# Second part of the query product units at later positions, one unit product ahead of the score tiles, two last-group steps joined

## The chip, the cores and the metric

The kernel runs on one core of one Trainium2 chip. The metric is the device time of one execution in microseconds (us). All times in this document are in us unless marked ns.

## What is computed

The inputs are x (2048 rows of 512), a key and a value cache for 32 heads of 128 columns, the projections wq (512 by 4096) and wo (4096 by 512), and the three weights of a gated block with 1792 inner columns. All are bf16.

```python
xn = layernorm(x)                                        # no scale, no offset
q  = (xn @ wq)   as 32 heads of 128
s  = softmax(q k_cache^T / sqrt(128)) @ v_cache          # all 2048 keys, no mask
s  = s as 2048 x 4096 @ wo
g  = silu((relu(xn @ W_gate) * (xn @ W_up)) @ W_down)
out = x + s * g
```

## The kernel before

**The main loop.** Attention is cut into 128 blocks: 32 heads (h) by 4 quarters of 512 query rows (Q), in that order. A block has 8 positions (p = 0 to 7). A position stands for one pair of key tiles, 256 keys. At each position TensorE (PE) runs two score tiles `S` (L1466, 128x512 each) of a pair three positions ahead, and eight products `PV` with the values (L1575, 128x129 each) of the present pair. ScalarE (ACT) turns each score pair into `PT` by one exp (L1478). The loop in L1761 to L1815 writes this out by hand: the order in which it emits instructions is the order in which each engine runs them, and nothing is reordered later. I write "block 26, position 4" as 26.4; as the loop is in L1762 to L1765, 26.4 emits the scores for the block position three further on (26.7) and the values of 26.4.

**The score ring.** `ps_r` has three slots of two PSUM banks. `ring_acquire` takes the slot at the front of the list, puts it at the back, and makes PE wait for the last reader of that slot. A score pair is read by its exp; another product by VectorE (DVE). A unit (below) holds a slot: the slot leaves the list until `ring_release` puts it back in second place, and meanwhile the score pairs rotate through the two others. The value products accumulate in `ps_acc`. At the end of a block DVE takes the reciprocal (L1495) and writes the normalized block (`Onorm`, L1498); the first value product of the next block waits for that.

**Other products at fixed positions.** `plan` maps (block, position) to groups of products that are emitted there between the score tiles and the value products. `side` does the same for work on other engines. What is in them in the part that the change touches:

- *Query product units* (`emit_unit`, L1019). From group 2 of four heads on, q is computed by a seven-product scheme of two nested levels. A unit is one outer product of one group; there are 7 units in each of 6 groups, 42 in all. Unit k of group g starts in block b = 16(g-1) + 5 + 2k and takes the outer products j = 1, 2, 6, 5, 3, 7, 4 in turn. It has six steps. Steps 0 to 3 stand in block b at positions 2, 3, 5, 6, or at 3, 4, 6, 7 where b is an "early" block; they hold one ring slot. Steps 4 and 5 are the second part: one 128x512 product each (L1032), at positions 2 and 4 of block b + 1, holding a slot again. Each product is added to sums by DVE (L1036, L1037).
- *Adds of a unit* (`add_unit`, L1095). After the second part of the units with j = 5 and j = 7, GpSimd (POOL) does four adds (L1103), which wait for the last DVE sum of that unit. The first DVE sum of the next unit's step 0 waits for these adds (`k.get("add")`, L1060, L1063), and PE's step 1 waits for that sum (L1066).
- *Preparation of a unit* (`prep_unit`, L992). POOL makes the eight sums that a unit multiplies; it waits for step 5 of the unit two before (`u_done`).
- *Output projection steps* (`emit_os`, L1326). 16 steps in the 16 blocks after each group, at position 0: three steps of two products, then a step of one product, four times over (each product is four 128x256 matmuls, L1347). DVE adds them to `s_acc` (L1363, L1365). The block of a one-product step is early (`early`, 24 such blocks in groups 2 to 7 that follow the second part of a unit, and 119): at position 0 PE emits the next two score pairs and then the step, which needs a third slot. Four DVE sums `OX` over SBUF (`emit_ox`, L1316 to L1324) serve four steps at a time; they stand at positions 2 to 5 of every eighth block, 24 and 32 for example.
- *The last group's steps* have been pulled together: steps 0 to 9 at blocks 112 to 121, steps 10 and 11 at 122.0 and 122.4, then 123.0, 124.0, 125.0 and 125.4. After each one-product step DVE finishes two sums (L1413, L1415), and `emit_base_next` (two DVE operations, L1443 and L1448) puts in the residual and g for each of 16 row tiles.

Of the kernel before, what the change touches and what calls it, by code (L numbers as in the profile page):

```python
# [30 lines left out]
def _wait(eng, tok):  # L31
    if tok is None:
        return
    sem, val = tok
    if val <= 0:
        return
    eng.wait_ge(sem.h, val)
# [15 lines left out]
def bass_recurrent_scan__mha_block_cached__glu_gated_reglu__prompt_kernel(  # L53
# [24 lines left out]
    NP = KT // 2  # L78
# [3 lines left out]
    NG = H // G  # L82
# [34 lines left out]
    with ExitStack() as es:  # L117
# [232 lines left out]
        def issue_wq(pr):  # L350
            b = pr % 2
            src = A_wq[:, pr * 2 * Dh:(pr + 1) * 2 * Dh].rearrange("(c p) e -> p c e", p=128)
            sem_wq[b].sig(sp.dma_start(Wq_sb[b][:].rearrange("p c i e -> p c (i e)"), src))
# [35 lines left out]
        def ring_acquire(hold=False):  # L389
            s = ring_order.pop(0)  # L390
            if not hold:
                ring_order.append(s)
            _wait_all(pe, ring_tok[s])
            ring_tok[s] = []
            return s
# [450 lines left out]
        def blk_of(gp):  # L846
            b, p = divmod(gp, NP)
            h, Q = divmod(b, QB)
            return b, h, Q, p

        def emit_M(items):
            if items[0][0] is emit_unit:
                emit_unit(*items[0][2:])
                return
            s = ring_acquire()
            toks = []
            k = 2 * s
            for fn, nb, *args in items:
                t = fn(*args, *range(k, k + nb))
                toks += t if isinstance(t, list) else [t]  # L860
                k += nb
            ring_tok[s] = toks
# [13 lines left out]
        def emit_st(pr, c, step, *banks):  # L876
# [57 lines left out]
            if c == 1:  # L934
# [6 lines left out]
        unit_at = [(g, j, GBK * (g - 1) + 5 + 2 * k) for g in range(2, NG)  # L941
                   for k, j in enumerate((1, 2, 6, 5, 3, 7, 4))]
        u_prep = {}
        u_done = {}
        u_tok = {}
        u_held = {}
# [338 lines left out]
        def emit_wx_scale(g):  # L1285
            W = Wo_sb[g % 2]
            _wait(pool, wo_tok(g))
            wflat = W[:].rearrange("p h d -> p (h d)")
            k = sem_wx.sig(pool.tensor_scalar(wflat, wflat, WOSC, None, op0=ALU.mult))
            wx_tok[(g, 0)] = k  # L1290
# [141 lines left out]
        def issue_xr(k):  # L1432
            n = base_order[k]
            if k >= 4:
                _wait(sp, base_done[base_order[k - 4]])
            sem_xr[k % 4].sig(sp.dma_start(xr_sb[:, k % 4:k % 4 + 1, :], x_t[:, n:n + 1, :]))
# [17 lines left out]
        def open_S_pair(gp):  # L1454
            b, h, Q, p = blk_of(gp)
            if p == 0:
                _wait(pe, qt_ready[(h, Q)])
                if Q == 0:
                    _wait(pe, kt_tok(h))
            s_slot[gp] = ring_acquire()  # L1460

        def emit_S_tile(gp, tt):
            b, h, Q, p = blk_of(gp)
            s = s_slot[gp]
            t = 2 * p + tt
            ins = pe.matmul(ps_r[:, 2 * s + tt, :], KT_sb[h % 2][:, t * 128:(t + 1) * 128],  # L1466
                            QT_sb[qt_slot[(h, Q)]][:], start=True, stop=True)
            if tt == 0:
                return
            stok = sem_s.sig(ins)  # L1470
            if p == NP - 1:
                qt_free.append((qt_slot[(h, Q)], stok))
                if Q == QB - 1:
                    shead_tok[h] = stok
            _wait(act, stok)
            pb = gp % NPB
            etok = sem_exp.sig(
                act.activation(PT[pb][:], ps_r[:, 2 * s:2 * s + 2, :], ACTF.Exp,  # L1478
                               scale=scale / WSC)
            )  # L1480
            assert etok[1] == gp + 1
            ring_tok[s] = [etok]
# [106 lines left out]
        def sp_head_start(h):  # L1589
            if h + 1 < H:  # L1590
                _wait(sp, shead_tok.get(h - 1))
                issue_kt(h + 1)
# [48 lines left out]
        def at(b, p, *items):  # L1641
            plan.setdefault((b, p), []).append(list(items))
# [4 lines left out]
        LB = NBLK - QB  # L1647
        side = {}
        osteps = {}
        early = set()  # L1650
        for g in range(NG - 1):
            b0 = (g + 1) * GB
            for i in range(16):
                it = (emit_os, 1 if i % 4 == 3 else 2, g, i // 4, i % 4)
                if g < NG - 2 or i < 10:
                    osteps[b0 + i] = it
                else:
                    at(b0 + (10, 10, 11, 12, 13, 13)[i - 10], 4 * (i in (11, 15)), it)
            for c in range(2):
                for i in range(4):  # L1660
                    side.setdefault((b0 + 7 * c, 1 + i) if c and g == NG - 2 else (b0 + 8 * c, 2 + i), []).append((emit_ox, g, c, i))
# [20 lines left out]
        for b in range(NBLK):  # L1682
            pr, r = (b - 2) // 8 + 1, (b - 2) % 8
# [22 lines left out]
            elif 0 < pr < NPR:  # L1706
                c, step = r // 4, r % 4
                q = (emit_st, 1 if step == 3 else 2, pr, c, step)
                first, second = (o, q) if step == 3 and o else (q, o)
# [4 lines left out]
                assert not o  # L1714
        for n, (g, j, b) in enumerate(unit_at):
            first = (3, 4, 6, 7) if b in early else (2, 3, 5, 6)
            for step, (r, p) in enumerate([(0, p) for p in first] + [(1, 2), (1, 4)]):
                at(b + r, p, (emit_unit, 0, n, step))
            side.setdefault((b - 2, 0), []).append((prep_unit, n))
            if j in (5, 7):  # L1720
                side.setdefault((b + 1, 5), []).append((add_unit, g, j))
        side.setdefault((GB + 1, 0), []).append((spill_g,))
        side.setdefault((LB - 9, 5), []).append((reload_g,))
        for g in range(2, NG):
            b = GB * (g - 1)
            side.setdefault((b + 2, 0), []).append((load_unit_w, g, 0))
            side.setdefault((b + 2, 6), []).append((scale_unit_w, g, 0))
            b, p = (21, 6) if g == 2 else (b + 4, 0)
            side.setdefault((b, p), []).append((load_unit_w, g, 1))
            b, p = (22, 4) if g == 2 else (b, 3)  # L1730
            side.setdefault((b, p), []).extend([(scale_unit_w, g, 1), (sum_unit_w, g)])
        base_at = [(LB - 7 + k // 2, 2 + k % 2) for k in range(4)]
        base_at += [(LB - 4 + k // 2, 2 + k % 2) for k in range(4)]
        base_at += [(LB - 1 + k // 2, 2 + k % 2) for k in range(4)]
        base_at += [(LB + 2, 2), (LB + 2, 5), (LB + 3, 1), (LB + 3, 3)]
        for bb, pp in base_at:
            side.setdefault((bb, pp), []).append((emit_base_next,))
# [6 lines left out]
        def emit_S_pair(gp):  # L1744
            open_S_pair(gp)
            emit_S_tile(gp, 0)
            emit_S_tile(gp, 1)
# [13 lines left out]
        for gp in range(LAG, TOTP):  # L1761
            gq = gp - LAG  # L1762
            bq, hq, Qq, pq = blk_of(gq)
            items = plan.pop((bq, pq), None)
            b, h, Q, p = blk_of(gp)  # L1765
            if p == 0 and Q == 0:
                sp_head_start(h)
            ahead = gp in s_ahead
            if not ahead:
                open_S_pair(gp)  # L1770
                emit_S_tile(gp, 0)
            if pq == 0 and bq % 8 == 4:
                pr = bq // 8 + 2
                if pr < 4:
                    _wait(sp, qp_done_tok[pr - 2])
                    issue_wq(pr)
            if pq == 4 and bq % 8 == 4:
                pr = bq // 8 + 2
                if pr < 4:
                    emit_sw(pr)  # L1780
            if pq == 0 and bq == (NG - 1) * GB + 4:
                _wait(sp, u_tok["last"])
                for k in range(4):
                    issue_xr(k)
            if pq == 4 and bq == 0:
                gu_sums(2)
            if pq == 0 and bq == 13:
                emit_wx_scale(0)
            if pq == 0 and bq == GB:
                emit_wx(0)  # L1790
            if pq == 0 and bq == GB + 4:
                emit_wx(1)
            if pq == 6 and bq % GB == 7 and 1 < bq // GB < NG - 1:
                emit_wx(bq // GB)
            if items:
                if not ahead:
                    emit_S_tile(gp, 1)
                if pq == 0 and bq in early:
                    s_ahead.add(gp + 1)
                    emit_S_pair(gp + 1)  # L1800
                for it in items:
                    emit_M(it)
            for fn, *args in side.pop((bq, pq), []):
                fn(*args)
            for fn in later.pop(gq, []):
                fn()
            now[0] = gq + 1
            split = not items and not ahead
            if split and (u_held or (pq == NP - 1 and bq + 1 in early)):
                emit_S_tile(gp, 1)  # L1810
                split = False
            emit_PV_tile(gq, 0)
            if split:
                emit_S_tile(gp, 1)
            emit_PV_tile(gq, 1)  # L1815
# [41 lines left out]
```

## Time and profile before

| what | value |
|---|---|
| median of 3 runs | 1254.27 (1254.26 to 1254.38) |
| the profiled execution's own time | 1254.29 |
| its span | 1252.9 |
| mean granted TensorE clock | 0.999 |
| PE matmul busy | 1233.0 (98%) |
| ACT busy | 1033.4 (82%) |
| DVE busy | 811.0 (65%) |
| POOL busy | 596.2 (48%) |

The span runs from the first to the last instruction of the program; the 1.4 us between span and time lie around it. A row of the timeline gives the start, the time from the first start to the last end, the engine, the line, what is written from what, and the count; in square brackets stands the idle time of that engine before it, with what ended it in the profiler's view. PEld is the loading of weights, which runs one matmul ahead of PE. A row of the waits gives who waited for whom, the sum, the count and the longest.

### The profile page before, as it was taken

The page shows a single profiled execution, that of the slowest core. Times are in us where ns is not written, and L with a number is a line of the kernel's source. Part 1 is how long each engine was busy: PE and PEld are TensorE (multiplying, and loading weights), DVE is VectorE, ACT ScalarE, POOL GpSimd, SP SyncE. Part 2 cuts the span into 40 slices and gives each one's busy share as a digit, 9 for nine tenths or more (in the row PEclk, how much of TensorE's full clock was granted, in tenths as well). Part 3 has the DMA queues.
Part 4 walks back from the last instruction along what each step waited for, and adds up shares of the span by engine and source line. Part 5 has one row for each costly group of instructions (what it writes and reads, how often), then busy time and mean ns, then how long its engine had stood idle before and what let it go on. Part 6 is the DMA issues. An engine that isn't in the chain of part 4 may idle for free.

```text
span 1252.9 us, 29140 instructions
## 1 busy us (share of the span) xinstructions
PE 1233.0 (98%) x12125; PEld 857.2 (68%) x12353; DVE 811.0 (65%) x1328; ACT 1033.4 (82%) x1109; POOL 596.2 (48%) x606
## 2 busy tenths in 40 slices
PE   9999999999999999999999999999999999999998
PEld 5466666776677676767667676667666776777775
DVE  7677877665576746575665747574666647674667
ACT  4457877668888898889898898889889898889994
POOL 3373876415734367344845366534835466430002
PEclk9999999999999999999999999999999999999999
DMA  9712331323122232323122333233222232235312
GB/s 273 155 31 39 77 77 23 54 45 107 43 48 52 69 65 52 52 64 69 41 38 39 72 61 51 48 69 68 48 51 49 45 58 48 52 64 144 76 35 77
DMA packets 254914, 82.25 MB, mean 66 GB/s; under 512 B 226368, under 2 KB 254784, under 8 KB 254784
## 3 DMA queue, kind: packets, MB, share of 16 engines
q1 hardware_dynamic: 254112, 79.98, 30.6%
q8 instruction: 98, 1.61, 0.5%
q10 hardware_dynamic: 672, 0.39, 0.1%
q14 instruction: 32, 0.26, 0.1%
HBM read 40.63 MB, written 4.19 MB: 36 GB/s over the span
## 4 chain that ended last, share of the span: by engine, by line
PE 80%; ACT 10%; issue 8%; DVE 1%; POOL 0%; DMA 0%; POOLq 0%; DVEq 0%
PE ps_acc L1575 31%; PE ps_r L1466 25%; ACT PT L1478 10%; PE ps_r L1347 6%; PE ps_r L1032 6%; PE ps_r L1144 3%; PE ps_r L1205 3%; PE ps_r L711 2%; PE ps_r L715 2%; PE ps_r L896 2%; PE ps_acc L814 1%; POOL g_sb L1630 0%; DMA x_sb<-in_A_x_dram 0%; PE ps_r L528 0%; DVE stats L406 0%
## 5 line engine op out<-in xcount | busy, mean ns | idle before, releaser
L1478 ACT ACTIVATE PT<-ps_r 128x1024 bf16<-128x1024 f32 x1024 | 982.0, 1030 | 150.4 <-PE ps_r L1466 142.4
L1575 PEld LDWEIGHTS ps_acc<-V_sb,PT 128*128 128x128 bf16 x8192 | 579.3, 98 | 202.4 <-ACT PT L1478 2.9
L1575 PE MATMUL ps_acc<-V_sb,PT 128*128 128x129 bf16 x8192 | 697.9, 220 | 5.6
L1466 PE MATMUL ps_r<-QT_sb,KT_sb 128*128 128x512 bf16 x1834 | 613.0, 379 | 5.0 <-DVE QT_sb L901 0.3
L1037 DVE TENSOR_TENSOR UVR<-UVR,ps_r 128x512 f32<-128x512 f32 (+1 forms) x228 | 166.3, 756 | 91.3 <-PE ps_r L1032 86.8
L1365 DVE TENSOR_TENSOR s_acc<-s_acc,ps_r 128x512 f32<-128x512 f32 x264 | 167.6, 682 | 21.5 <-PE ps_r L1347 21.5
L1466 PEld LDWEIGHTS ps_r<-QT_sb,KT_sb 128*128 128x128 bf16 x2048 | 175.6, 98 | 7.6 <-ACT PT L1478 0.5
L1495 DVE RECIPROCAL rz_sb<-ps_acc 128x4 f32<-128x4 f32 x127 | 23.0, 181 | 186.2 <-PE ps_acc L1575 185.3
L1498 DVE TENSOR_TENSOR Onorm<-ps_acc,rz_sb 128x512 bf16<-128x512 f32 x127 | 87.8, 692 | 4.4
L1004 POOL TENSOR_TENSOR TI<-xn_sb 128x512 f16<-128x512 f16 x48 | 58.0, 1209 | 68.0 <-PE ps_r L1032 68.0
L978 POOL TENSOR_SCALAR Wq_sb<-Wq_sb 128x1024 bf16<-128x1024 bf16 x12 | 33.2, 2769 | 118.3 <-DMA Wq_sb<-in_A_wq_dram 118.3
L1037 DVE TENSOR_TENSOR QT_sb<-UVR,ps_r 128x512 bf16<-128x512 f32 x72 | 49.5, 688 | 36.2 <-PE ps_r L1032 33.2
L1004 POOL TENSOR_TENSOR TI<-xnT 128x512 f16<-128x512 bf16 x36 | 41.6, 1156 | 64.2 <-PE ps_r L1032 63.4
L1103 POOL TENSOR_TENSOR QT_sb<-UVR,UVR 128x512 bf16<-128x512 f32 x24 | 34.8, 1481 | 72.7 <-DVE UVR L1037 72.7
L1630 POOL TENSOR_TENSOR g_sb<-s_acc,WX 128x512 bf16<-128x512 f32 x6 | 6.8, 1154 | 124.1 <-DVE WX L1623 124.1
L1103 POOL TENSOR_TENSOR UVR<-UVR,UVR 128x512 f32<-128x512 f32 x24 | 29.7, 1269 | 72.6 <-DVE UVR L1037 72.6
L1004 POOL TENSOR_TENSOR TI<-xn_sb,TI 128x512 f16<-128x512 f16 x48 | 55.3, 1152 | 0.0
L1032 PE MATMUL ps_r<-TI,SI 128*128 128x512 f16 x126 | 48.2, 382 | 0.6
L1347 PE MATMUL ps_r<-WX,OX 128*128 128x256 f16 x336 | 45.8, 273 | 0.0
L1004 POOL TENSOR_TENSOR TI<-xnT,TI 128x512 f16<-128x512 bf16 x36 | 41.6, 1156 | 0.0
L1120 POOL TENSOR_SCALAR gB<-gB 128x512 bf16<-128x512 bf16 x14 | 20.8, 1487 | 42.6 <-DVE gB L1150 42.6
L1347 PEld LDWEIGHTS ps_r<-WX,OX 128*128 128x128 f16 x336 | 32.8, 98 | 9.8 <-ACT PT L1478 1.8
(186 smaller groups left out, 1193.9 us busy)
## 6 DMA issues: line engine op xcount, KB each, us to landing
V_sb<-in_A_v_cache_dram SPq DMA_DIRECT2D x32, 512.0 KB, 4.3
Wq_sb<-in_A_wq_dram SPq DMA_DIRECT2D x16, 256.0 KB, 3.1
Wo_sb<-in_A_wo_dram SPq DMA_DIRECT2D x8, 512.0 KB, 4.1
out_dram<-g_sb SPq DMA_DIRECT2D x4, 512.0 KB, 4.8
g_sb<-out_dram SPq DMA_DIRECT2D x4, 512.0 KB, 6.4
xr_sb<-in_A_x_dram SPq DMA_DIRECT2D x16, 128.0 KB, 2.2
OT_store<-Onorm SPq DMA_TRANSPOSE x127, 2.5
Wd_sb<-in_B_W_down_dram SPq DMA_DIRECT2D x1, 1792.0 KB, 14.0
```

The source lines that it names most:

```text
L1004: return sem_ui.sig(pool.tensor_tensor(dst, x, y, o))
L1032: return sem_up.sig(pe.matmul(dst, lhs, rhs, start=start, stop=stop, skip_group_check=True))
L1037: dve.tensor_tensor(dst, x, ps, ALU.add))
L1103: u_tok["add"] = sem_uv.sig(pool.tensor_tensor(dst, UU[:, i, :], RR[:, i, :], ALU.add))
L1144: ins = pe.matmul(ps_r[:, bank, :], L(i), R(i), start=(i == 0), stop=(i == HC - 1))
L1205: ins = pe.matmul(ps_r[:, bank, j * DH:(j + 1) * DH], L(i), R(i), start=(i == 0 and j == 0), stop=(i == HF - 1 and j == 1))
L1347: ins = pe.matmul(ps_r[:, bank, j * DH:(j + 1) * DH], L(i), R(i), start=(i == 0 and j == 0), stop=(i == GH - 1 and j == 1))
L1365: t = dve.tensor_tensor(names[k], names[k], view(bank), op)
L1466: ins = pe.matmul(ps_r[:, 2 * s + tt, :], KT_sb[h % 2][:, t * 128:(t + 1) * 128], QT_sb[qt_slot[(h, Q)]][:], start=True, stop=True)
L1478: act.activation(PT[pb][:], ps_r[:, 2 * s:2 * s + 2, :], ACTF.Exp, scale=scale / WSC)
L1498: dve.tensor_tensor(Onorm[ob][:], o_ap, rz_sb[:].to_broadcast([128, 4, Dh]), ALU.mult))
L1575: ins = pe.matmul(o_ap, PT[pb][:, tt, j * 128:(j + 1) * 128], V_sb[vb][:, t, 0:VW], start=(t == 0 and j % 2 == 0), stop=(t == KT - 1 and j ...
```

## The change

1. The second part of each unit (steps 4 and 5) moves from positions 2 and 4 of block b + 1 to 5 and 7 where b + 2 is early, and to 3 and 5 elsewhere.
2. In early blocks that begin a unit, step 3 (position 7) is emitted before the score tiles of that position, not after them. The score pair there is then split around the value products like a plain one.
3. In the last group, the one-product step 7 no longer has block 119 to itself. Steps 8 to 10 move one block earlier, and step 7 is emitted with the one-product step 11 at 122.0 in one slot. Block 119 is thereby no longer early. Eight of the 16 `emit_base_next` calls move with them: from 120.2, 120.3, 121.2, 121.3, 123.2, 123.3, 124.2, 124.3 to 122.3, 122.5, 123.2, 123.3, 123.5, 124.2, 124.3, 124.5.

No instruction is added or taken away.

```diff
+        ahead_of_S = set()
...
             for i in range(16):
                 it = (emit_os, 1 if i % 4 == 3 else 2, g, i // 4, i % 4)
-                if g < NG - 2 or i < 10:
-                    osteps[b0 + i] = it
+                k = (0, 1, 2, 3, 4, 5, 6, None, 7, 8, 9, 10, 11, 12, 13, 13)[i] if g == NG - 2 else i
+                if k is None:
+                    late = it
+                elif g < NG - 2 or i < 10:
+                    osteps[b0 + k] = it
                 else:
-                    at(b0 + (10, 10, 11, 12, 13, 13)[i - 10], 4 * (i in (11, 15)), it)
+                    at(b0 + k, 4 * (i == 15), *([late] if i == 11 else []), it)
...
             first = (3, 4, 6, 7) if b in early else (2, 3, 5, 6)
-            for step, (r, p) in enumerate([(0, p) for p in first] + [(1, 2), (1, 4)]):
+            second = (5, 7) if b + 2 in early else (3, 5)
+            for step, (r, p) in enumerate([(0, p) for p in first] + [(1, p) for p in second]):
                 at(b + r, p, (emit_unit, 0, n, step))
+            if first[3] == NP - 1:
+                ahead_of_S.add(b)
...
-        base_at += [(LB - 4 + k // 2, 2 + k % 2) for k in range(4)]
-        base_at += [(LB - 1 + k // 2, 2 + k % 2) for k in range(4)]
+        base_at += [(LB - 2, 3), (LB - 2, 5), (LB - 1, 2), (LB - 1, 3), (LB - 1, 5), (LB, 2), (LB, 3), (LB, 5)]
...
             ahead = gp in s_ahead
+            if pq == NP - 1 and bq in ahead_of_S:
+                for it in items:
+                    emit_M(it)
+                items = None
             if not ahead:
                 open_S_pair(gp)
                 emit_S_tile(gp, 0)
```

## The prediction

> **What bounds the kernel now.** I read the page first (busy shares, chain), then the waits, then the timeline of single block boundaries.
>
> ```profile
> PE 1233.0 (98%) x12125; PEld 857.2 (68%) x12353; DVE 811.0 (65%) x1328; ACT 1033.4 (82%) x1109; POOL 596.2 (48%) x606
> PE 80%; ACT 10%; issue 8%; DVE 1%; POOL 0%; DMA 0%; POOLq 0%; DVEq 0%
> PEld ps_r L1347 <- ACT PT L1478: 18.4, 43, 0.7
> ```
>
> PE is busy for 98% of the span, and no matmul is removed. So only PE's short waits can move the time. The largest in the changed part is the third row: 43 times the weights of an output projection step wait for an exp, because the step's ring slot still holds a score pair. The sum of 18.4 overstates it, since weights load one matmul ahead. What PE itself loses is read at one boundary, 26 to 27:
>
> ```profile
> 372.76 0.59 PE L1466 MATMUL ps_r<-QT_sb,KT_sb 128*128 128x512 bf16 x2
> 373.20 0.62 PE L1575 MATMUL ps_acc<-V_sb,PT 128*128 128x129 bf16 x8
> 373.65 1.03 PE L1466 MATMUL ps_r<-QT_sb,KT_sb 128*128 128x512 bf16 x4
> 374.76 0.61 PE L1347 MATMUL ps_r<-WX,OT_store 128*128 128x256 f16 x4
> 375.21 0.28 PE L1575 MATMUL ps_acc<-V_sb,PT 128*128 128x129 bf16 x2
> ...
> 373.85 0.18 DVE L1495 RECIPROCAL rz_sb<-ps_acc 128x4 f32<-128x4 f32 x1 [2.42 <-PE ps_acc L1575]
> 374.07 0.69 DVE L1498 TENSOR_TENSOR Onorm<-ps_acc,rz_sb 128x512 bf16<-128x512 f32 x1
> ...
> 367.88 3.77 ACT L1478 ACTIVATE PT<-ps_r 128x1024 bf16<-128x1024 f32 x4 [0.70 <-PE ps_r L1466]
> 371.85 3.77 ACT L1478 ACTIVATE PT<-ps_r 128x1024 bf16<-128x1024 f32 x4 [0.20 <-PE ps_r L1466]
> ...
> 370.33 0.38 PE L1032 MATMUL ps_r<-TI,SO 128*128 128x512 f16 x1
> 370.74 0.69 DVE L1037 TENSOR_TENSOR UVR<-UVR,ps_r 128x512 f32<-128x512 f32 x1 [1.30 <-PE ps_r L1032]
> ```
>
> Rates first. Four score tiles take 1.03 and a single 512-column matmul 0.38, so one streams for (1.03 - 0.38)/3 = 0.217. Eight value products stream for 373.65 - 373.20 = 0.45. A pair of tiles plus its values is thus 0.88, while exps in a row come every (3.77 - 1.04)/3 = 0.91: ACT falls a little behind wherever no extra product stands. From 373.20 to 375.21 PE did 0.45 + 4 x 0.217 = 1.32 and four 256-column matmuls (0.44, see below), together 1.76, in 2.01. So 0.25 is lost at each early boundary. There are 24 behind a unit's second part: 6.0 us in all, the most that moving it can win there.
>
> **The early boundary (blocks 22, 26, 30, 34 of each group; 24 cases).** Step 5 now stands at 26.7 before the values. The score pair of 26.7 comes one product earlier (372.54 for 372.76), step 5 follows at 372.98, and the values stay at 373.20: moving costs nothing by itself, and the exp that the projection step needs (third of the row at 371.85, ending 371.85 + 2 x 0.91 + 1.04 = 374.71) ends some 0.3 earlier. Three waits take its place.
> (a) From 26.5 to 26.7 the unit holds a slot. The pair of 26.6 then needs the exp of 26.7's scores, the fourth of the row at 367.88, ending 371.65. With 0.05 for the semaphore (374.71 to 374.76 above) PE gets it at 371.70, and wants it at 371.66 (372.54 less 0.88); the next pair waits some 0.03 more by ACT's 0.91. Together 0.07.
> (b) The second score pair of 27.0 takes the slot that step 5 gave back, so it waits for DVE: 0.41 to DVE's start (370.33 to 370.74), 0.69 and 0.05, 1.15 after step 5. PE arrives after one product, eight values and two score tiles: 0.217 + 0.45 + 0.43 = 1.10. Wait 0.05.
> (c) That DVE sum also holds back the reciprocal, and the first values of 27.0 wait for Onorm, which ends 0.9 after the reciprocal can start: another 0.04.
> So 0.25 becomes 0.16: gain 0.09, times 24 = 2.2 us. Ends: nothing (ACT a little slower) and the whole 6.0.
>
> **Step 3 ahead of the score tiles (18 cases).**
>
> ```profile
> 381.91 0.38 PE L1032 MATMUL ps_r<-xn_sb,SO 128*128 128x512 f16 x1
> 382.13 0.62 PE L1575 MATMUL ps_acc<-V_sb,PT 128*128 128x129 bf16 x8
> 382.58 0.59 PE L1466 MATMUL ps_r<-QT_sb,KT_sb 128*128 128x512 bf16 x2
> 383.08 1.05 PE L1347 MATMUL ps_r<-Wo_sb,OT_store 128*128 128x256 bf16 x8
> 383.98 0.22 PE L1575 MATMUL ps_acc<-V_sb,PT 128*128 128x129 bf16 x1
> ...
> 382.33 0.69 DVE L1036 COPY UVR<-ps_r 128x512 f32<-128x512 f32 x1 [0.41 <-PE ps_r L1032]
> 383.14 0.69 DVE L1498 TENSOR_TENSOR Onorm<-ps_acc,rz_sb 128x512 bf16<-128x512 f32 x1
> ...
> 383.07 0.77 PEld L1347 LDWEIGHTS ps_r<-Wo_sb,OT_store 128*128 128x128 bf16 x8 [0.39 <-DVE UVR L1036]
> ```
>
> A 256-column matmul streams for (1.05 - 0.61)/4 = 0.11. From step 3 (381.91) to 383.98 PE did 0.217 + 0.45 + 0.43 + 0.87 = 1.97 in 2.07: 0.10 lost, because the projection step takes the slot that step 3 released and DVE ends at 383.02. After the change step 3 is 0.43 earlier, but the ring turns with it: the slot now goes to the first score pair of 28.0. Between step 3 and that pair stand one product, two score tiles and eight values, again 1.10 against 1.15. The wait stays; only Onorm comes free a little sooner. I take 0.03 x 18 = 0.5 us gained, between 0.9 lost and 1.8 gained (the whole 0.10).
>
> **Second part at 3 and 5 (18 cases): the held slot.** No row shows this wait, but (a) is the nearest. At 28.5 the pair needs the exp of the pair of 28.3, and by 0.91 a piece ACT is one exp behind: 0.02 x 18 = 0.4 us lost, between 0 and 0.1 each.
>
> **Who waits for step 5.** No DMA is issued by these steps. `prep_unit` and the weight loads on SP wait for step 5 too, but they are wanted a block and more later. The adds are not: they start when step 5's DVE sum ends, now one position (0.88) later, and DVE's first sum of the next unit stands still behind them.
>
> ```profile
> 423.05 0.69 DVE L1037 TENSOR_TENSOR UVR<-UVR,ps_r 128x512 f32<-128x512 f32 x1
> 423.65 0.68 DVE L1321 TENSOR_TENSOR OX<-OX,OT_store 128x1024 f16<-128x1024 f16 x1
> 424.37 1.65 DVE L1324 TENSOR_TENSOR OX<-OT_store,OX 128x1024 f16<-128x1024 bf16 x1
> ...
> 429.71 0.69 DVE L1037 TENSOR_TENSOR UVR<-UVR,ps_r 128x512 f32<-128x512 f32 x1 [1.40 <-PE ps_r L1032]
> ...
> 423.81 5.80 POOL L1103 TENSOR_TENSOR QT_sb<-UVR,UVR 128x512 bf16<-128x512 f32 x4 [12.11 <-DVE UVR L1037]
> ...
> 429.25 0.38 PE L1032 MATMUL ps_r<-TI,SI 128*128 128x512 f16 x1
> ...
> 430.45 0.10 PEld L1032 LDWEIGHTS ps_r<-TI,SI 128*128 128x128 f16 x1 [0.44 <-DVE UVR L1037]
> ...
> 388.92 4.95 POOL L1103 TENSOR_TENSOR UVR<-UVR,UVR 128x512 f32<-128x512 f32 x4 [12.10 <-DVE UVR L1037]
> ...
> 394.77 0.69 DVE L1037 TENSOR_TENSOR UVR<-UVR,ps_r 128x512 f32<-128x512 f32 x1 [1.35 <-PE ps_r L1032]
> ```
>
> For j = 7 (block 32) the adds end at 423.81 + 5.80 = 429.61 and DVE starts 0.10 later, at 429.71. The profile names PE for that idle time, but PE's product was at 429.25 and DVE follows in 0.41, at 429.66: both end the wait, and there is no slack. Step 1 is wanted at 429.25 + 1.10 = 430.35 and comes at 430.45. So each further delay is PE's in full, at six places. How long the adds take when moved: 5.80 beside two OX sums, 4.95 for the same four adds with none (row at 388.92). Step 5 now stands between those OX sums, so the third is done before the adds and only the fourth lies beside them. I take 5.4, halfway: 424.69 + 5.4 + 0.10 = 430.19, later by 0.48, less the 0.02 that PE is later: 0.45 x 6 = 2.7 us lost. Ends: 0 (4.95) and 0.86 x 6 = 5.2 (5.80).
> The Trainium skill, "SBUF — State Buffer", section "Who interferes with whom", states that a DVE operation with two SBUF inputs and a GpSimd operation that reads SBUF exclude each other, and that the one issued first holds the port to its end. The 1.65 of the OX sum at 424.37 against 0.68 for the one at 423.65 agrees. By that rule the fourth OX sum, starting at 424.54, holds the adds from 424.69 to 425.23, and they take about 5.5; shared in proportion, the adds and the sums would both stretch and 5.80 could stay.
> For j = 5 (block 28) the adds end at 393.87; 0.88 later they end at 394.75, DVE starts at 394.85 where PE's product lets it at 394.79: 0.07 x 6 = 0.4 us, between 0 and 0.5.
>
> **The last group.**
>
> ```profile
> 1164.84 0.62 PE L1575 MATMUL ps_acc<-V_sb,PT 128*128 128x129 bf16 x8
> 1165.29 1.03 PE L1466 MATMUL ps_r<-QT_sb,KT_sb 128*128 128x512 bf16 x4
> 1166.53 0.61 PE L1347 MATMUL ps_r<-WX,OT_store 128*128 128x256 f16 x4 [0.21 <-ACT PT L1478]
> 1166.98 0.39 PE L1575 MATMUL ps_acc<-V_sb,PT 128*128 128x129 bf16 x4
> ...
> 1189.31 0.18 DVE L1495 RECIPROCAL rz_sb<-ps_acc 128x4 f32<-128x4 f32 x1 [3.14 <-PE ps_acc L1575]
> ...
> 1190.17 1.88 DVE L1365 TENSOR_TENSOR s_acc<-s_acc,ps_r 128x512 f32<-128x512 f32 x3
> ...
> 1195.91 0.69 DVE L1413 TENSOR_TENSOR s_acc<-s_acc 128x512 f32<-128x512 f32 x1
> 1196.63 0.69 DVE L1415 TENSOR_TENSOR s_acc<-s_acc 128x512 f32<-128x512 f32 x1
> 1197.69 0.18 DVE L1495 RECIPROCAL rz_sb<-ps_acc 128x4 f32<-128x4 f32 x1 [0.37 <-PE ps_acc L1575]
> ```
>
> Block 119 is no longer early: 2.14 - 1.76 = 0.38 gained. But block 122 gets DVE work: from one reciprocal to the next 0.86 to the sums, four sums (0.60 each), four of finishing and four of base (0.7 each), 8.9, while PE's block lasts 8.38 less the 0.44 of the step that left, 7.94. The reciprocal, and the values behind it, come some 0.9 late. Net 0.5 lost, between 0.4 gained and 0.6 lost.
>
> **Sum.** Lost 2.7 + 0.4 + 0.4 + 0.5 = 4.0; gained 2.2 + 0.5 = 2.7. Net +1.3 on the profiled execution's 1254.29 (span 1252.9 and 1.4 around it; the median is 0.02 lower): 1255.6. A measurement of this kernel can tell about 0.2%, 2.5 us, from no change.
>
> **The rivals.**
> - *Slower*: the adds keep 5.80. Then 5.2 stands for 2.7, net +3.8, 1258.1. It decides from 0.65 a place, adds of 5.6. For it: DVE's start follows the adds' end in 0.10. Against: only one OX sum beside them. With the early boundary at no gain, 1260. Chance of over 0.2% slower, 0.34.
> - *Faster*: the waits (a) to (c) and the one at step 3 vanish wholly: 6.0 + 1.8 stands for 2.7, net -3.8, 1250.5. For it: the exp ends 0.3 earlier. Against: 1.15 against 1.10 from rows. Chance 0.14.
> - *Within 0.2%*: the forecast, 0.52. The parts cancel; its own range is 1252.5 to 1256.8.
>
> The range 1252.0 to 1259.0 takes in most of the slower case and the near end of the faster.
>
> **What would show it.** In the profile after: the early boundary from values to values 1.9 for 2.01, its projection step no longer behind ACT; step 1 of the j = 4 units idle 0.8 to 0.9 for 0.44, the adds near 5.4; a late reciprocal at the end of block 122. I am wrong if step 1 shows no longer idle time, or if the weight loads of the projection steps still wait for exps 43 times.

## The result and the profile after

| | before | after |
|---|---|---|
| median, us (lowest to highest of 5 runs each, same chip) | 1254.27 (1254.07 to 1254.38) | 1260.13 (1259.99 to 1260.47) |
| the profiled execution's own time | 1254.29 | 1260.08 |
| span | 1252.9 | 1258.7 |
| mean granted TensorE clock | 0.999 | 1.0 |

The ratio is 1.0047, with an interval of 1.0032 to 1.0062: slower by 5.9 us, and 1.1 beyond the upper end of the predicted range. Between the two profiled executions lie 5.8 us.

Line numbers behind the change are one higher in after: L1348, L1467 and L1576 are the projection, score and value products that were L1347, L1466 and L1575. From the page of after come the busy time of the engines and the chain, and from its waits three rows (who waited for whom: sum, count, longest). The last row of the block is from the waits of before, for comparison with the third; a row like the fifth does not stand in before. In the timelines below, rows that the text doesn't use are left out.

```profile
PE 1237.9 (98%) x12130; PEld 860.1 (68%) x12353; DVE 809.6 (64%) x1328; ACT 1031.1 (82%) x1109; POOL 597.0 (47%) x606
PE 80%; ACT 9%; issue 8%; DVE 2%; POOL 0%; DMA 0%; DVEq 0%; POOLq 0%
PEld ps_r L1033 <- DVE UVR L1038: 15.0, 30, 0.9
PEld ps_r L1348 <- ACT PT L1479: 4.2, 20, 0.2
PEld ps_r L1467 <- DVE UVR L1038: 5.1, 13, 0.4
PEld ps_r L1032 <- DVE UVR L1037: 12.0, 30, 0.4
```

The waits of the projection steps for exps did go, from 43 times and 18.4 to 20 times and 4.2. But the share of the chain that ACT lost went to DVE (ACT had 10% and DVE 1% in before): score pairs now wait for DVE sums, and the longest wait of a unit product for DVE is 0.9, against 0.4 in before.

**Where the 5.8 us are.** Each value product of after was set beside the same product of before. Each has a time at which its weights load, and the difference of these two times was followed through the trace. Where the difference rises, after loses. It changes at few places, and alike each time (with rounding the rows add up to 5.95):

| place | each | times | sum | the prediction |
|---|---|---|---|---|
| early boundary (27.0 and its like) | -0.17 at 12, -0.10 at 12 | 24 | -3.1 | with the next row -2.2 |
| the slot held before it (26.6, 26.7) | +0.09 | 24 | +2.1 | |
| slot held from 3 to 5 (28.5) | +0.10 | 18 | +1.8 | +0.4 |
| step 1 behind the late adds of j = 7 (33.3) | +0.43 | 6 | +2.6 | +2.7 |
| step 1 behind the late adds of j = 5 (29.3) | +0.08 | 6 | +0.5 | +0.4 |
| blocks 40, 56, 72, 88, 104 (40.7) | +0.36 | 5 | +1.8 | nothing |
| step 3 ahead of the score tiles | -0.02, once +0.34 | 17 and 1 | +0.05 | -0.5 |
| last group (119, 122, 123) | -0.39, +0.09, +0.47 | 1 | +0.2 | +0.5 |

**The early boundary.** From the timeline of after, the boundary 26 to 27 that the prediction showed of before:

```profile
373.07 0.38 PE L1033 MATMUL ps_r<-TI,SO 128*128 128x512 f16 x1
373.29 0.62 PE L1576 MATMUL ps_acc<-V_sb,PT 128*128 128x129 bf16 x8
373.49 0.69 DVE L1038 TENSOR_TENSOR UVR<-UVR,ps_r 128x512 f32<-128x512 f32 x1 [1.39 <-PE ps_r L1033]
373.75 1.10 PE L1467 MATMUL ps_r<-QT_sb,KT_sb 128*128 128x512 bf16 x4
374.10 0.17 DVE L1496 RECIPROCAL rz_sb<-ps_acc 128x4 f32<-128x4 f32 x1
374.23 0.11 PEld L1467 LDWEIGHTS ps_r<-QT_sb,KT_sb 128*128 128x128 bf16 x2 [0.39 <-DVE UVR L1038]
374.31 0.69 DVE L1499 TENSOR_TENSOR Onorm<-ps_acc,rz_sb 128x512 bf16<-128x512 f32 x1
374.68 0.60 PE L1348 MATMUL ps_r<-WX,OT_store 128*128 128x256 f16 x4
375.11 0.92 PEld L1576 LDWEIGHTS ps_acc<-V_sb,PT 128*128 128x128 bf16 x16
375.14 1.51 PE L1576 MATMUL ps_acc<-V_sb,PT 128*128 128x129 bf16 x20
```

From values to values PE took 375.14 - 373.29 = 1.85 where before took 2.01. The projection step follows the score tiles with no wait, as forecast. In its place stand the two DVE waits of the prediction: the second score pair loads 0.05 after step 5's sum ends (374.18 to 374.23), and the reciprocal, which in before began 0.03 after the values' end, begins at 374.10 for 373.94. Onorm ends at 375.00 and the next values load 0.11 later. So DVE's sum of step 5 at position 7 sets this boundary now; the run with step 5 at 6, below, tests that.

**The late adds.** The timeline at blocks 32 and 33 in after:

```profile
424.10 0.69 DVE L1038 TENSOR_TENSOR UVR<-UVR,ps_r 128x512 f32<-128x512 f32 x1 [0.20 <-PE ps_r L1033]
424.71 0.68 DVE L1325 TENSOR_TENSOR OX<-OT_store,OX 128x1024 f16<-128x1024 bf16 x1
424.87 5.35 POOL L1104 TENSOR_TENSOR QT_sb<-UVR,UVR 128x512 bf16<-128x512 f32 x4 [10.32 <-DVE UVR L1038]
430.30 3.14 DVE L1038 TENSOR_TENSOR UVR<-UVR,ps_r 128x512 f32<-128x512 f32 x4 [1.82 <-PE ps_r L1033]
431.04 0.10 PEld L1033 LDWEIGHTS ps_r<-TI,SI 128*128 128x128 f16 x1 [0.86 <-DVE UVR L1038]
```

The adds take 5.35, DVE starts 0.08 behind their end, and step 1's weights idle 0.86 for 0.44. This went as the prediction said, to the tenth. The fourth OX sum (424.71) was issued ahead of the adds and kept its 0.68.

**Blocks 40 and its like, not foreseen.** Step 5 of the unit in block 38, POOL and DVE in before, from its timeline:

```profile
473.39 0.38 PE L1032 MATMUL ps_r<-TI,Wq_sb 128*128 128x512 f16 x1
473.85 1.16 POOL L1004 TENSOR_TENSOR TI<-xn_sb 128x512 f16<-128x512 f16 x1 [3.41 <-PE ps_r L1032]
488.87 1.16 POOL L1305 TENSOR_TENSOR WX<-WX,Wo_sb 128x512 f16<-128x512 f16 x1
489.98 0.69 DVE L1316 TENSOR_TENSOR OX<-OT_store 128x1024 f16<-128x1024 bf16 x1
491.36 0.69 DVE L1037 TENSOR_TENSOR QT_sb<-UVR,ps_r 128x512 bf16<-128x512 f32 x1
```

and the same in after:

```profile
476.72 0.38 PE L1033 MATMUL ps_r<-TI,Wq_sb 128*128 128x512 f16 x1
477.18 1.15 POOL L1005 TENSOR_TENSOR TI<-xn_sb 128x512 f16<-128x512 f16 x1 [5.80 <-PE ps_r L1033]
489.85 1.61 POOL L1302 TENSOR_TENSOR WX<-Wo_sb 128x512 f16<-128x512 bf16 x1
491.43 1.61 POOL L1304 TENSOR_TENSOR WX<-Wo_sb,WX 128x512 f16<-128x512 bf16 x1
489.16 1.28 DVE L1317 TENSOR_TENSOR OX<-OT_store 128x1024 f16<-128x1024 bf16 x1
491.35 0.68 DVE L1319 TENSOR_TENSOR OX<-OT_store 128x1024 f16<-128x1024 bf16 x1
491.95 1.64 DVE L1322 TENSOR_TENSOR OX<-OX,OT_store 128x1024 f16<-128x1024 f16 x1
493.51 0.68 DVE L1038 TENSOR_TENSOR QT_sb<-UVR,ps_r 128x512 bf16<-128x512 f32 x1
494.24 0.10 PEld L1467 LDWEIGHTS ps_r<-QT_sb,KT_sb 128*128 128x128 bf16 x1 [0.36 <-DVE QT_sb L1038]
```

`prep_unit` starts on POOL 0.46 after step 5 in both, so it starts 3.3 later in after; some 0.5 of this is what the whole program is late by then. What it makes is wanted late, but POOL is a queue, and the four WX sums (weights for a later group's projection, L1300 to L1305) stand behind it. In before the last of them ended at 490.03, just as DVE's first OX sum began at 489.98, so nothing was spare. In after they lie beside the OX sums. An OX sum took 0.69 beside none; here two of them take 1.28 and 1.64, and DVE's sum of step 5 in block 40, which stands behind these in DVE's queue, comes too late for the score pair that wants its slot, and PE waits 0.36. The two engines took turns: the WX sum queued at 491.43 ended at 493.04, 1.0 after the OX sum at 491.35 had, and the OX sum issued at 491.95 ended 0.55 after that.
The Trainium skill, "SBUF — State Buffer", section "Who interferes with whom", calls the port that DVE with two SBUF inputs shares with GpSimd an exclusive lock; these turns agree with it. That it is this port, no run here shows.

### The profile page after: what moved, and what is told of

Its sections match the earlier page's. It is cut to its first block, busy times and chain, and to the rows that moved or that the text cites. A ratio compares the mean times of both kernels' runs of the same rounds, so it can differ in the third digit from the quotient of the medians.

```text
span 1258.7 us, 29145 instructions
## 1 busy us (share of the span) xinstructions
PE 1237.9 (98%) x12130; PEld 860.1 (68%) x12353; DVE 809.6 (64%) x1328; ACT 1031.1 (82%) x1109; POOL 597.0 (47%) x606
## 3 DMA queue, kind: packets, MB, share of 16 engines
q8 instruction: 98, 1.61, 0.6%
## 4 chain that ended last, share of the span: by engine, by line
PE 80%; ACT 9%; issue 8%; DVE 2%; POOL 0%; DMA 0%; DVEq 0%; POOLq 0%
PE ps_acc L1576 30%; PE ps_r L1467 27%; ACT PT L1479 9%; PE ps_r L1348 5%; PE ps_r L1033 5%; PE ps_r L1145 3%; PE ps_r L1206 3%; PE ps_r L711 2%; PE ps_r L715 2%; PE ps_r L896 2%; PE ps_acc L814 1%; DVE UVR L1038 1%; DVE QT_sb L1038 1%; POOL g_sb L1631 0%; DVE OX L1322 0%
## 5 line engine op out<-in xcount | busy, mean ns | idle before, releaser
L1576 PEld LDWEIGHTS ps_acc<-V_sb,PT 128*128 128x128 bf16 x8192 | 582.7, 98 | 211.0 <-ACT PT L1479 3.4
L1576 PE MATMUL ps_acc<-V_sb,PT 128*128 128x129 bf16 x8192 | 705.3, 220 | 7.2 <-DVE Onorm L1499 0.3
L1467 PE MATMUL ps_r<-QT_sb,KT_sb 128*128 128x512 bf16 x1835 | 619.1, 380 | 5.8 <-DVE QT_sb L1038 0.9
L1467 PEld LDWEIGHTS ps_r<-QT_sb,KT_sb 128*128 128x128 bf16 x2048 | 173.2, 98 | 19.4 <-DVE QT_sb L1038 7.3
L1631 POOL TENSOR_TENSOR g_sb<-s_acc,WX 128x512 bf16<-128x512 f32 x6 | 6.8, 1154 | 124.2 <-DVE WX L1624 124.2
L1104 POOL TENSOR_TENSOR QT_sb<-UVR,UVR 128x512 bf16<-128x512 f32 x24 | 32.1, 1367 | 62.3 <-DVE UVR L1038 62.3
L1348 PE MATMUL ps_r<-WX,OX 128*128 128x256 f16 x336 | 45.8, 273 | 0.0
L1348 PEld LDWEIGHTS ps_r<-WX,OX 128*128 128x128 f16 x336 | 32.9, 98 | 9.8 <-ACT PT L1479 1.8
```

The source lines that it names most:

```text
L1104: u_tok["add"] = sem_uv.sig(pool.tensor_tensor(dst, UU[:, i, :], RR[:, i, :], ALU.add))
L1348: ins = pe.matmul(ps_r[:, bank, j * DH:(j + 1) * DH], L(i), R(i), start=(i == 0 and j == 0), stop=(i == GH - 1 and j == 1))
L1576: ins = pe.matmul(o_ap, PT[pb][:, tt, j * 128:(j + 1) * 128], V_sb[vb][:, t, 0:VW], start=(t == 0 and j % 2 == 0), stop=(t == KT - 1 and j ...
```

## The experiments

All medians stand beside runs of the kernel before on the same chip (medians 1254.16 to 1254.27). "Trace" means the differences against before, place by place, as in the table above.

**Which part loses: second part at 3 and 5 alone.** To before:

```diff
-            for step, (r, p) in enumerate([(0, p) for p in first] + [(1, 2), (1, 4)]):
+            second = (2, 4) if b + 2 in early else (3, 5)
+            for step, (r, p) in enumerate([(0, p) for p in first] + [(1, p) for p in second]):
```

> The kernel before, with one part of the change: the second part of the units begun in early blocks at positions 3 and 5 of their block (for 2 and 4); all else as before. Theory (the loss is that step 5 comes late for the work queued behind its DVE sum): the trace after loses 0.10 at each of 18 held slots, 0.36 at 5 places where step 5's sum stands behind the OX sums, 0.43 at 6 places behind the j = 7 adds and 0.08 at 6 behind the j = 5 adds, together 6.6: 1260.9 us. Rival (the loss sits at the early boundaries and in the turned ring of score slots, not here): 1254 to 1255.5.

Measured 1259.18, ratio 1.0039 (1.0026 to 1.0051). Trace: 0.10 at 18 places, 0.42 at 6, 0.09 at 6, together 4.9, and nothing at block 40. So the held slot and the adds are real and belong to this move; the third loss does not come with this move alone. The theory's 1260.9 was too high, because it put the loss of block 40 here.

**The rest alone: those units back at 2 and 4.** To after:

```diff
-            second = (5, 7) if b + 2 in early else (3, 5)
+            second = (5, 7) if b + 2 in early else (2, 4)
```

> The changed kernel, with that one part undone: second part of the units begun in early blocks at 2 and 4 again, at 5 and 7 before early blocks, step 3 ahead of the score tiles, last group joined. Theory: the same 6.6 go, 1253.5 us, a little faster than before (early boundary 1.0 gained, last group 0.2 lost). Rival: 1259 to 1260.

Measured 1259.92, ratio 1.0045 (1.0032 to 1.0058). The theory fell, and this run told why: the losses at 28.5, 29.3 and 33.3 are gone, but blocks 40, 56, 72, 88 and 104 now lose 0.89 at position 6 and 0.40 at the end, 6.4 in all. With step 5 of their own unit at position 4 instead of 5, DVE's sum for it stands behind two stretched OX sums (1.11 and 1.64 in block 40 of this run). So the two parts are not additive: each hides some of what the other exposes.

**The adds alone.** To after:

```diff
+            second = (5, 7) if b + 2 in early else (2, 4) if j == 7 else (3, 5)
```

> The changed kernel with only the j = 7 units (one a group, 6 in all) back at 2 and 4. Theory that the adds are the largest single loss: 6 x (0.43 + 0.10) = 3.2 less, 1256.9 us, with step 1 of the next unit at 0.44 of idle weight loading again. Rival (the adds are covered elsewhere and the held slot is the price): 6 x 0.10 = 0.6 less, 1259.5.

Measured 1257.0, ratio 1.0022 (1.0013 to 1.0031): the 6 units with j = 7 are worth 3.1 us of the 5.9, as the theory said (0.43 by the adds and 0.10 by the held slot, times 6).

**The collision on POOL and DVE.** To after, the WX sums at the same position two blocks later:

```diff
-            if pq == 6 and bq % GB == 7 and 1 < bq // GB < NG - 1:
+            if pq == 6 and bq % GB == 9 and 1 < bq // GB < NG - 1:
```

> The changed kernel with the GpSimd sums of the output weights (WX) of groups 2 to 6 two blocks later, so that none lies beside the OX sums of blocks 40, 56, 72, 88 and 104. Theory (those OX sums stand ahead of step 5's sum on DVE and are stretched from 0.68 to 1.64 by the WX sums on GpSimd): 5 x 0.36 = 1.8 less, 1258.3 us, the OX sums at 0.7 again. Rival (being queued behind the OX sums is enough, GpSimd has no part): no change, 1260.1.

Measured 1258.35, ratio 1.0034 (1.0022 to 1.0047), 1.8 less than after, as the theory said. Trace against after: the 0.36 at 40.7 and its four like goes, the 0.10 of the held slot stays, and from block 2 on no other place differs by more than 0.02. The execution of this trace took 1259.41; its extra 1.1 lies ahead of block 2, where both kernels are alike. The OX sum that took 1.64 at 491.95 in after is in this run

```profile
493.05 0.68 DVE L1322 TENSOR_TENSOR OX<-OX,OT_store 128x1024 f16<-128x1024 f16 x1
```

So the WX sums beside the OX sums are the cause of this loss; behind OX sums of 0.68 step 5's sum is in time (in this run DVE idles 0.20 ahead of it, at 493.92).

**The early boundary by itself.** To before, with the WX sums two blocks later as above:

```diff
+            second = (5, 7) if b + 2 in early else (2, 4)
```

> The kernel before with one part of the change alone, the second part at 5 and 7 ahead of early blocks, and the WX sums two blocks later as well, so that they do not fall beside the OX sums. Theory: the part gains what the trace of after shows, 0.13 at each of 24 early boundaries, and pays 0.09 for the slot held from 5 to 7: 24 x 0.04 = 1.0 gained, 1253.3, and no loss at blocks 40, 56, 72, 88, 104. Rival one, the prediction's own figure of 2.2: 1252.1. Rival two, the loss at those five blocks has another cause than the WX sums: 1255 to 1259.

Measured 1253.32, ratio 0.9992 (0.9983 to 1.0001), by itself at the edge of what can be measured; the trace gives -0.9: 12 x 0.17 and 12 x 0.10 gained, 24 x 0.09 lost to the held slot, and no loss at block 40. The theory's figure, not the prediction's 2.2.

**The same, one position earlier.** As before it, but

```diff
+            second = (4, 6) if b + 2 in early else (2, 4)
```

> As the run before it, but with the second part at 4 and 6 ahead of early blocks. Theory: in after it is DVE's sum of step 5 at position 7 that holds back the reciprocal and through it the first values of the next block; at 6 that sum ends a position earlier, while ACT still gets the one product of time that lets the projection step's exp end early. So the boundary gains 0.25 instead of 0.13, the held slot costs 0.05 instead of 0.09, as ACT lags less there: 24 x 0.2 = 4.8 gained, 1249.5. Rival: the exp of the projection step's slot then ends the wait again, the boundary gains no more than 0.13: 1252.5 or above.

Measured 1250.3, ratio 0.9969 (0.9958 to 0.9981). The timeline of this run at the boundary 26 to 27:

```profile
372.32 0.69 DVE L1037 TENSOR_TENSOR UVR<-UVR,ps_r 128x512 f32<-128x512 f32 x1 [1.40 <-PE ps_r L1032]
373.00 0.62 PE L1575 MATMUL ps_acc<-V_sb,PT 128*128 128x129 bf16 x8
373.66 0.18 DVE L1495 RECIPROCAL rz_sb<-ps_acc 128x4 f32<-128x4 f32 x1 [0.65 <-PE ps_acc L1575]
374.28 0.36 PEld L1347 LDWEIGHTS ps_r<-WX,OT_store 128*128 128x128 bf16 x4 [0.29 <-ACT PT L1478]
374.76 1.07 PE L1575 MATMUL ps_acc<-V_sb,PT 128*128 128x129 bf16 x16
```

Values to values take 374.76 - 373.00 = 1.76, the whole sum of PE's work there. DVE has finished step 5 at 373.01 and is idle when the reciprocal comes. The trace gives 0.26 gained at each of 24 boundaries and 0.10 lost to the held slot, 3.8 of the 4.1 in all; the theory had 0.25 and 0.05. So it was DVE's sum at position 7 that ate the gain of the change, and the held slot costs 0.1 here too.

**The last group, with its base sums respread.** To before, the last-group part of the change, and

```diff
-        base_at += [(LB - 2, 3), (LB - 2, 5), (LB - 1, 2), (LB - 1, 3), (LB - 1, 5), (LB, 2), (LB, 3), (LB, 5)]
+        base_at += [(LB - 2, 5)] + [(LB - 1, p) for p in (1, 2, 3)] + [(LB, p) for p in (1, 2, 3, 5)]
```

> The kernel before with the last-group part of the change alone, and with the eight base sums respread: from 122.3 122.5 123.2 123.3 123.5 124.2 124.3 124.5 to 122.5 123.1 123.2 123.3 124.1 124.2 124.3 124.5, so that DVE has one of them in block 122 instead of two. Theory: the gain of 0.4 at block 119 stays and the loss of 0.6 at the ends of blocks 122 and 123, where the reciprocal waits behind DVE's sums, shrinks: 0.2 to 0.4 gained in all, 1253.9 to 1254.1, and the reciprocal at the end of block 122 no longer late. Rival: the sums come late wherever they stand, 1254.4 to 1254.7.

Measured 1253.94, ratio 0.9998 (0.9989 to 1.0007): inside the theory's 1253.9 to 1254.1, though the ratio alone can't be told from 1; the trace has -0.39 at 119, +0.09 at 122 and nothing at 123. DVE at the end of block 122, in after and then in this run:

```profile
1195.01 0.18 DVE L1496 RECIPROCAL rz_sb<-ps_acc 128x4 f32<-128x4 f32 x1 [5.20 <-PE ps_acc L1576]
1195.87 2.48 DVE L1366 TENSOR_TENSOR s_acc<-s_acc,ps_r 128x512 f32<-128x512 f32 x4
1198.27 0.68 DVE L1414 TENSOR_TENSOR s_acc<-s_acc 128x512 f32<-128x512 f32 x1
1202.97 0.69 DVE L1449 TENSOR_TENSOR s_acc<-s_acc,xr_sb 128x512 f32<-128x512 f32 x1
1203.58 0.17 DVE L1496 RECIPROCAL rz_sb<-ps_acc 128x4 f32<-128x4 f32 x1
```

```profile
1195.99 0.69 DVE L1448 TENSOR_TENSOR s_acc<-s_acc,xr_sb 128x512 f32<-128x512 f32 x1
1197.39 0.18 DVE L1495 RECIPROCAL rz_sb<-ps_acc 128x4 f32<-128x4 f32 x1 [0.71 <-PE ps_acc L1575]
```

In after the reciprocal follows DVE's last sum with no idle time; here it has 0.71 to spare.

**Step 3 behind the score tiles again.** From after:

```diff
-            if first[3] == NP - 1:
-                ahead_of_S.add(b)
```

> After without its second item: step 3 at position 7 is emitted behind the score tiles again. Theory: that item is worth nothing at 17 of its 18 places and costs 0.35 at block 47, so this kernel takes 1259.8, and PE is 0.3 to 0.4 earlier from block 48 on. Rival, the prediction's 0.03 gained at each place: 1260.6.

Measured 1260.04, ratio 1.0046 (1.0033 to 1.006), not to be told from after. Trace: the loss of 0.34 at 48.0 goes, as the theory said, and the 17 gains of 0.02, 0.3 in all, go with it; the theory had these at nothing. The item is worth nothing on balance.

**The parts that gained, together.** Before with 4 and 6 ahead of early blocks, the WX sums two blocks later, and the last group respread:

> The kernel before with the second part at 4 and 6 ahead of early blocks (2 and 4 elsewhere), the WX sums two blocks later, and the last group joined with its base sums respread: the parts that gained, together. Theory: they touch different blocks, so the gains add, 3.9 and 0.3: 1250.0. Rival: the gains overlap or the sums of one disturb the other, 1250.5 or above.

Measured 1250.21 (1249.95 to 1250.45), ratio 0.9968 (0.9956 to 0.9981): faster than before by 4.0 us and than after by 9.9. This lies between the theory's 1250.0 and the rival's 1250.5. The trace gives -3.95; the last group's 0.3 is below what the medians tell.

**Without moving the WX sums.** Before with 4 and 6 and nothing else:

> The kernel before with the second part at 4 and 6 ahead of early blocks and nothing else, the WX sums where they were. Theory: step 5 at 38.6 rather than 38.4 starts the preparation on POOL some 2.0 later, the WX sums behind it move by as much and the last two of them fall beside OX sums of block 40; the sum of step 5 there comes up to 0.9 late at five places: 1250.3 + 5 x (0.2 to 0.9) = 1251.3 to 1254.8, and the loss stands in blocks 40, 56, 72, 88, 104 only. Rival, a shift of 2.0 is still covered: 1250.3.

Measured 1256.3, ratio 1.0017 (1.0007 to 1.0026). The one line of the WX sums decides between 3.9 us faster and 2.1 slower. The trace loses 1.20 at 40.6 and its four like, 6.0 in all. The place and the cause are those of the theory, but the size lies above its 0.2 to 0.9, so that the time missed its 1251.3 to 1254.8. POOL, DVE and PE's weights in block 40 of this run:

```profile
488.97 1.16 POOL L1303 TENSOR_TENSOR WX<-Wo_sb,WX 128x512 f16<-128x512 bf16 x1
490.20 1.48 POOL L1305 TENSOR_TENSOR WX<-WX,Wo_sb 128x512 f16<-128x512 f16 x1
489.25 1.42 DVE L1316 TENSOR_TENSOR OX<-OT_store 128x1024 f16<-128x1024 bf16 x1
490.59 1.64 DVE L1318 TENSOR_TENSOR OX<-OT_store 128x1024 f16<-128x1024 bf16 x1
492.15 0.68 DVE L1037 TENSOR_TENSOR QT_sb<-UVR,ps_r 128x512 bf16<-128x512 f32 x1
492.88 0.10 PEld L1466 LDWEIGHTS ps_r<-QT_sb,KT_sb 128*128 128x128 bf16 x1 [1.20 <-DVE QT_sb L1037]
```

The two OX sums ahead of step 5's sum are stretched by 0.7 and 0.95, and PE waits 1.20 for the slot that this sum gives back.

## Why the prediction was wrong

It forecast a net loss of 1.3 and got 5.8. The 1260 that its slower rival names at the far end is near the measured 1260.1 by luck: it rests on adds of 5.80, which took 5.35. By the prediction's own steps:

- **Who waits for step 5: the step that failed outright.** "`prep_unit` and the weight loads on SP wait for step 5 too, but they are wanted a block and more later." What `prep_unit` makes is indeed wanted late, and so are the WX sums; but they stand behind it in POOL's queue and move with it, and the prediction did not ask beside what they would fall. Moving step 5 from 38.4 to 38.7 moved POOL's queue, the WX sums met the OX sums, and 1.8 us were lost (6 in the runs with that move where step 5 stands at 4 in blocks 40 and the like). Shown by the run with the WX sums later and by the pair of runs at 4 and 6.
- **The held slot at 3 and 5, mis-sized.** Forecast 0.02 each with an upper end of 0.1, measured 0.10 at 18 places: 1.8 for 0.4. The prediction set ACT's lag alone against the wait. In after's timeline at 28.5,

```profile
385.20 4.69 ACT L1479 ACTIVATE PT<-ps_r 128x1024 bf16<-128x1024 f32 x5 [0.78 <-PE ps_r L1467]
387.64 0.62 PE L1576 MATMUL ps_acc<-V_sb,PT 128*128 128x129 bf16 x8
388.17 0.13 PEld L1467 LDWEIGHTS ps_r<-QT_sb,KT_sb 128*128 128x128 bf16 x2
388.20 0.59 PE L1467 MATMUL ps_r<-QT_sb,KT_sb 128*128 128x512 bf16 x2
```

  the exps come every (4.69 - 1.03)/4 = 0.915, so the third ends at 385.20 + 2 x 0.915 + 1.03 = 388.06. The weights load 0.11 after that, not 0.05, and PE, whose eight values are through at 387.64 + 0.45 = 388.09, starts at 388.20. The pair emitted at 28.5 is the first of block 29, and so is the pair that loses 0.10 at 26.5 in the runs at 4 and 6; later pairs of a block lose 0.06 and 0.03. The trace shows where the extra 0.06 goes. The load of a first pair has a wait for DVE too (its query tile), long met here. The wait for the exp then stands in an instruction of its own ahead of the load (EVENT_SEMAPHORE in PE's queue, 388.09 to 388.14; the timelines leave such instructions out), while the load of a later pair carries it itself.
- **The early boundary, half right.** The mechanism held: the exp is no longer waited for, and waits (a), (b) and (c) came. Their sizes were 0.09, 0.05 and 0.16 late for the reciprocal. At half of the places (j = 1 and 6) 0.08 were gained on balance, near the forecast 0.09; at the other half (j = 3 and 4, whose step 5 writes the query tile) nothing. In after's timeline at the boundary 30 to 31,

```profile
408.06 0.38 PE L1033 MATMUL ps_r<-TI,SO 128*128 128x512 f16 x1
408.54 0.69 DVE L1038 TENSOR_TENSOR QT_sb<-UVR,ps_r 128x512 bf16<-128x512 f32 x1 [1.39 <-PE ps_r L1033]
```

  DVE's sum starts 0.48 after the product; at 26.7 (373.07, 373.49) it was 0.42. Here too the trace shows an instruction that only waits (408.476 to 408.497): the sum that writes the query tile has a second wait, for PE's score products. In before, all 48 sums of this kind that waited for their product started 0.49 behind the start of the product and have such an instruction ahead of them; the 95 at L1037 that write `UVR` have none, and their median is 0.42. In all 1.0 for 2.2.
- **Step 3 ahead of the tiles: nothing for 0.5.** The wait stayed, as argued, and the gain was 0.02 for 0.03; one place (48.0) lost 0.34; why that one is open. The prediction looked at one place of 18.
- **The adds: right.** 0.43 for 0.45 at j = 7, 0.08 for 0.07 at j = 5; the adds took 5.35 for 5.4. The slower rival, adds at 5.80, did not happen. Slower it was, but not by that way.
- **The last group: sign right, 0.2 for 0.5.** The late reciprocal came where it was said. Its DVE work took 1203.58 - 1195.01 = 8.57, not 8.9: sums in a row come every 0.66 ((1203.58 - 1198.27)/8), and the prediction took 0.7.

Set together: the collision +1.8, the held slot +1.4, the early boundary +1.2, step 3 +0.55, less 0.4 of the last group and the adds, is the 4.5 between forecast and trace.

## What to carry to other kernels

Before a step is moved, walk down the queue of every engine that waits for it, to the work standing behind the waiting instruction, and ask beside what that work will then fall; here a queue with nothing to spare turned a gain of 3.9 us into a loss of 2.1. Place a product that is to give another engine time one step before the boundary, not on it, so that the sum it needs does not stand ahead of the boundary's own. And when a wait is seen at one place of many, check it at several: half of the early boundaries and one of the 18 moved steps behaved otherwise.

## What was not expected of the hardware

An OX sum on DVE, 0.68 by itself, took up to 1.64 beside a POOL sum, and the POOL sum 1.61 for 1.16. Neither engine is short of time (DVE is busy for 64% of the span, POOL for 47%), and yet this delays a third, PE, by 1.2 in one place. And a second wait came with a delay. Where an instruction had two, one stood in an instruction of its own ahead of it, and it started later, a weight load 0.11 after the exp's end for 0.05, a DVE sum 0.49 after the start of its product for 0.42.
